# Two heads' scores in neighbouring PSUM banks with one sigmoid for both, the first mixing's products with U in four column groups, and a new table of places

## The chip, the cores and the metric

The kernel runs on one core of one Trainium2 chip, in one launch. A core has a matrix engine (TensorE, PE in the profile, with its weight loads as PEld), VectorE (DVE), ScalarE (ACT), GpSimd (POOL) and SyncE (SP), which here only issues transfers. Each engine works through its own queue in the order in which the program puts the instructions there. The metric is the device time of one execution in microseconds; lower is better. The execution that was profiled is one of its own, so its time stands beside the median of the timed runs.

## The reference, cut to what matters

Sigmoid attention for 8 samples, 12 heads of 64, 448 positions, and behind it a mixing over positions of rank 32 and a feed-forward with 768 and 3072 channels:

```python
scores = scale * np.matmul(q, k.transpose(0, 1, 3, 2)) - np.log(S)
attn = 1.0 / (1.0 + np.exp(-scores))
x = np.matmul(attn, v)              # heads side by side: 8 x 448 x 768
h = xt @ U @ V                      # xt: positions last; U 448x32, V 32x448
u = x + h.transpose(0, 2, 1)
out = u + np.maximum(u @ w_ch1, 0.0) @ w_ch2
```

The two feed-forward weights come as 64-bit words and are decoded on the chip.

## The kernel before, in words

Data lie with channels or heads on the partitions and the 448 positions along the free side. The work of a sample has three stages.

**Attention.** `pair` (line 569) takes two heads at a time, six pairs a sample. `scores_of` (L521) multiplies k and q: the two heads lie on rows 0 to 63 and 64 to 127, so that their products (L533) run in two halves of the matrix engine's rows, side by side. Each head's block of 128 keys by 448 queries fills its own PSUM bank. ScalarE drains each bank with a sigmoid of its own (L649, called in a loop over two heads at L671). `values_of` (L543) multiplies with v (L552, L562), the two heads in two halves of the columns. Samples 0 and 1 (`whole`) do this in f32. The later six, in the order of `LATER`, split every operand into two f16 parts; the attention matrix is then scaled into an f16 high part (ACT, L679) and a low part (VectorE, L680, shown by its helper's line L393).

**Mixing.** `mix(0)` (L707) serves sample 0 in f32. It transposes u by the matrix engine (L736), copies the result into one of the two buffers `XN` (ACT, L747), multiplies it with a 128-row piece of U (L748: four pieces, added up in one bank's partitions 0 to 31), copies the sum out (L765) and multiplies it with V (L773). Then u is scaled and split into `us0` (`u_parts`, L788), which is the feed-forward's input.

**Feed-forward.** Four samples run it plainly: chains of 18 products (`ffn_in`, L914), two relu drains on ACT (L921, L922) and a subtraction on VectorE (L923), then chains of 12 products (`ffn_out`, L933), each drained by one VectorE addition into u (L940, in the profile L393 with `ua`). The other four go through a Strassen-like scheme, two samples at once (L1117).

While sample 0 is in its feed-forward, `decode` (L854) turns the weights into f16 parts. A piece of 768 KB is loaded into one of the three `W64` buffers, goes through two or three VectorE operations (L393, L390), on ACT through L442 for most groups, then through an absolute sum on ACT (`bound`, L453), which gives the buffer back, and at last through a scaling on ACT or GpSimd and a subtraction on VectorE. Four pieces make a group, twelve groups make both weights.

**What sets the order.** `Plan.order` (L130) plays the program through with a cost for every operation and writes the order in which each engine gets its instructions. Among the operations that could start, the one with the smallest `pos` goes first. The positions come from the constants of lines 60 to 69. A position only sets preference: nothing waits for it.

**PSUM.** There are 8 banks of 512 f32. The feed-forward takes from banks 0 to 2 (`PF`, L320), attention from banks 3 to 7 (`PS_`); sample 0 and the first two pairs of sample 1 take scores from all eight.

Of the kernel before, what the change touches and what calls it, by code (L numbers as in the profile page):

```python
# [26 lines left out]
F32 = mybir.dt.float32  # L27
# [11 lines left out]
P = 128  # L39
D = 64  # L40
S = 448
NP = 6
RANK = 32
# [13 lines left out]
FORMS = {1: (0,), 2: (1,), 3: (2,)}  # L57
MM = 0.1893
SWITCH, BOND = 0.11, 6.0
PIPE, LANDS, LATE = 0.33e6, 3.237, 0.855  # L60

ROOM0, ROOM, AHEAD, BEFORE, PACE = 71.122, 36.236, 46.443, 36.513, 0.773
PREP, BOUNDS, VALUES, SECOND, MIXED = 17.173, 9.225, -1.615, 1.701, 4.481
MIXED1, MIX_1 = 5.441, 15.09
MIX_2, EV_IN, EV_OUT, A_OFF = 11.033, 27.459, 4.648, 3.832
START, DECODE = 67.28, 39.505
U_AT, U_STEP = 4.035, 4.181
LEAD, SUMS, STEP_K, STEP_I, FFN_LEAD = 13.145, 6.985, 47.972, 26.851, 5.28
W_AT, W_STEP, PAIR0, MIX0A, MIX0B, W2_LAG, G0_LEAD = -159.513, 5.093, 4.16, -122.622, -80.644, 0.581, 0.562
LOW_G = 1  # L70
ORDER = "iiiioiooiioiooiioiooiooo"

# [159 lines left out]
def fused_kernel(ctx: ExitStack, tc: tile.TileContext, q, k, v, wu, wv, w1, w2, out):  # L232
# [78 lines left out]
    for x, owners in ((stg, None), (at_.bitcast(F16), AT2), (US[1].ap.rearrange("p a b c -> p (a b c)"), US[1:])):  # L311
        for j in range(min(4, x.shape[1] // (2 * PIECE))):
# [3 lines left out]
                t.shares.append(o)  # L316
                o.shares.append(t)
            T32.append(t)
    BANK = [Buffer(ps.tile([P, 512], F32, name=f"bank{i}")) for i in range(8)]
    PF, PS_ = [BANK[:3]] * B, [BANK[3:]] * B  # L320
    ROW = ring("row", 1, [3 * P], F32)

    SPOT = []
# [61 lines left out]
    def pe(cost, fn, reads, writes, pos, slack=None, after=(), modes=(128, 128)):  # L385
        return op("PE", cost, fn, reads, writes, pos, LATE if slack is None else slack, 0.3, after, modes=modes)
# [118 lines left out]
    def rows_of(h):  # L505
        return slice(h * D, h * D + D)
# [14 lines left out]
    def scores_of(b, js, products, kp, pos, early):  # L521


        sc = {(j, h): plan.tile("sc", BANK if early else PS_[b], False) for j in js for h in range(2)}
        n = 1 if b < WHOLE else 3

        def fn():
            for j in js:
                for i in range(n):
                    for h in range(2):  # L530
                        if j < 3:
                            x, y = products[-1]()[i]
                            nc.tensor.matmul(sc[j, h].x[:, :S], x[rows_of(h), j * P : j * P + P], y[rows_of(h)], start=i == 0, stop=i == n - 1)  # L533
                            continue
                        for m in range(2):
                            x, y = products[m]()[i]
                            nc.tensor.matmul(sc[j, h].x[rows_of(m), :S], x[rows_of(h), 3 * P : S], y[rows_of(h)], start=i == 0, stop=i == n - 1)  # L537

        scored.append(pe(len(js) * (0.74 if b < WHOLE else 0.57) + (SWITCH if 3 in js and len(js) > 1 else 0.0), fn, kp, list(sc.values()), pos,
                         after=values_ops[-2:-1] + scored[-1:], modes=(32 if js[0] == 3 else 64, 32 if js[-1] == 3 else 64)))  # L540
        return sc

    def values_of(b, products, tiles, kp, pos, quad):  # L543
        av = plan.tile("av", PS_[b], False)
        avs = [quad["av"], av] if quad else [av]

        def fn():
            n = len(products())
            for j in range(3):
                for i, (x, y) in enumerate(products()):  # L550
                    for h in range(2):
                        nc.tensor.matmul(  # L552
                            av.x[rows_of(h), :S], x[:, j, rows_of(h)], y(tiles[j], h),
                            start=j == 0 and i == 0, stop=not quad and j == 2 and i == n - 1, skip_group_check=True,
                        )
            if not quad:
                return
            for i in range(n):
                for m in range(2):
                    x, y = quad["last"][m]()[i]  # L560
                    for h in range(2):
                        nc.tensor.matmul(avs[m].x[rows_of(h), :S], x[rows_of(m), rows_of(h)], y(tiles[3], h)[rows_of(m)],  # L562
                                         start=False, stop=i == n - 1, skip_group_check=True)

        three, one = (2.22, 0.74) if b < WHOLE else (1.71, 0.57)
        values_ops.append(pe(three + (SWITCH + one if quad else 0.0), fn, kp, avs, pos, modes=(65, 32 if quad else 65)))
        return av

    def pair(b, p, at, d):
# [92 lines left out]
        for j in range(3 + odd):  # L662
            here = at + (d * (j // 2) / SECOND if b else 0.0)
            kj = kscore + (quad["kscore"] if odd and (j == 3 or b and j == 2) else [])
            if b == 0:
                sc = scores_of(b, (j,), products, kj, here, early)
            elif j % 2 == 0:
                sc = scores_of(b, (j, j + 1) if j == 0 or odd else (j,), products, kj, here, early)
            a = tiles[j] = plan.tile("a2", A2)
            to = a if whole else plan.tile("t2", AT2)  # L670
            for h in range(2):  # L671
                cols = slice(h * S, h * S + S)
                sigmoid(0.66 if whole else 0.72, lambda to=to, cols=cols: to.x[:, cols],
                        lambda h=h, sc=sc, j=j: sc[j, h].x[:, :S], c if j < 3 or whole else cm, here, [sc[j, h]], [(to, h)])
            kto = [(to, h) for h in range(2)]
            if whole:
                keys += kto
                continue
            act(0.95, lambda a=a, to=to: nc.scalar.activation(half(a, 0), to.x, AF.Copy, scale=A_UP), kto, [(a, 0)], here + A_OFF)  # L679
            dve2(1.16, lambda a=a, to=to: rest(half(a, 1), to.x, A_UP, half(a, 0)), kto + [(a, 0)], [(a, 1)], here + A_OFF)  # L680
            keys += [(a, 0), (a, 1)]
# [25 lines left out]
    def mix(b, pos0, pos1):  # L707
# [18 lines left out]
        for hf in range(2):  # L726
# [3 lines left out]
            for sc in range(4):  # L730
# [12 lines left out]
                if whole:  # L743
                    def x32(xn=xn, w=w):
                        return xn.x.rearrange("p a b -> p (a b)").bitcast(F32)[:w]

                    act(0.48, lambda tr=tr, w=w, x32=x32: nc.scalar.copy(x32(), tr.x[:w, :384]), [tr], [xn], at)  # L747
                    pe(0.66, lambda tp=tp, w=w, sc=sc, x32=x32: nc.tensor.matmul(  # L748
                        tp.x[:RANK, :384], uraw[:w, sc], x32(), start=sc == 0, stop=sc == 3), [xn, "uraw"], [tp], at)
                    continue  # L750
                act(0.58, lambda tr=tr, xn=xn, w=w: nc.scalar.activation(xn.x[:w, 0, :], tr.x[:w, :384], AF.Copy, scale=sx.x[:w]),
                    [tr, sx], [(xn, 0)], at)
# [9 lines left out]

                pe(0.34, mixed, [(xn, 0), (xn, 1)] + KUA, [tp], at)
            if whole:
                act(0.5, lambda tp=tp, half=half: nc.scalar.copy(tt.x[:RANK, half], tp.x[:RANK, :384]), [tp], [(tt, hf)], at)  # L765
            else:
                to_t16(tp, hf, at)
        at = pos1 + (0.0 if whole else MIX_1)
        for c in range(NP):
            cut = slice(c * P, (c + 1) * P)  # L770
            lp = plan.tile("sc", BANK if b == 0 else PS_[b], False)
            if whole:
                pe(4 * MM, lambda lp=lp, cut=cut: nc.tensor.matmul(lp.x[:, :S], tt.x[:RANK, cut], vraw[:RANK], start=True, stop=True),  # L773
                   [(tt, c // 3), "vraw"], [lp], at)
                dve(0.62, lambda lp=lp, c=c: nc.vector.tensor_add(u32[c].x, lp.x[:, :S], u32[c].x), [lp, ku[c]], [ku[c]], at)
            else:
# [601 lines left out]
```

## Time and profile before

| what | us |
|---|---|
| median of 3 runs | 1550.19 (1549.12 to 1557.4) |
| the profiled execution | 1549.95 |
| its span in the profile | 1548.2 |
| TensorE matmul busy | 1526.8 |
| VectorE busy | 1119.3 |
| ScalarE busy | 846.2 |
| GpSimd busy | 388.1 |

The span runs from the first to the last instruction that the profiler saw; the profiled execution's time is 1.75 us longer. Busy time is the union of the instructions on an engine. A matmul's duration includes its way through the array, so that a chain of matmuls at 358 ns each still starts one every 189 ns; the idle time in brackets and the granted clock tell more than the busy share.

### The profile page before, as it was taken

How to read it: one execution, taken by the hardware profiler on the slowest of the kernel's cores; microseconds unless marked ns; L12 is line 12 of the kernel's file. 1: busy time of each engine (PE TensorE's matmuls, PEld its weight loads, DVE VectorE, ACT ScalarE, POOL GpSimd, SP SyncE). 2: the span in 40 equal slices, each digit the busy share in tenths (PEclk: the TensorE clock that was granted, in tenths of full speed). 3: DMA queues.
4: the chain of work that ended last, by engine and by line, in shares of the span. 5: the costliest groups of instructions: out<-in, count | busy, mean ns of one | idle time of the engine just before them, and what ended most of it. 6: DMA issues, size and time to landing. Idle time of an engine off the chain costs nothing.

```text
span 1548.2 us, 24076 instructions
## 1 busy us (share of the span) xinstructions
PE 1526.8 (99%) x8843; PEld 751.5 (49%) x8843; DVE 1119.3 (72%) x1864; ACT 846.2 (55%) x1495; POOL 388.1 (25%) x538
## 2 busy tenths in 40 slices
PE   8999989999999999999999999999999999999999
PEld 3344544544444444444444454555555555555554
DVE  4687998568776777867788757697866777565656
ACT  6788956368767667857689536342332614131310
POOL 1000010552223362323332441046454500000000
PEclk9999999999999999999999999999999999999999
DMA  8877867685664775755766566967575673443331
GB/s 235 276 264 256 293 239 256 247 257 168 178 172 130 238 205 173 203 142 149 221 205 193 181 210 217 296 204 264 179 249 170 226 257 108 122 128 108 107 108 72
DMA packets 184726, 306.02 MB, mean 198 GB/s; under 512 B 54560, under 2 KB 146080, under 8 KB 178464
## 3 DMA queue, kind: packets, MB, share of 16 engines
q1 hardware_dynamic: 184608, 304.49, 62.4%
q8 instruction: 69, 1.13, 0.3%
q14 instruction: 49, 0.40, 0.1%
HBM read 232.88 MB, written 63.26 MB: 191 GB/s over the span
## 4 chain that ended last, share of the span: by engine, by line
PE 90%; DMA 3%; DVE 3%; ACT 2%; issue 1%; SPq 0%; ACTq 0%
PE bank L1117 37%; PE bank L933 19%; PE bank L914 19%; PE bank L533 6%; PE bank L552 6%; DMA w<-w_in 1%; PE bank L562 1%; PE bank L537 1%; PE bank L829 1%; DMA qk__99<-q_in 1%; DMA v__105<-v_in 1%; ACT a L649 1%; DVE us__88 L393 1%; PE bank L838 0%; ACT w L453 0%
## 5 line engine op out<-in xcount | busy, mean ns | idle before, releaser
L933 PE MATMUL bank<-h__93,w__91 128*128 128x448 f16 x792 | 162.4, 358 | 6.5 <-DVE ua__77 L393 3.0
L933 PE MATMUL bank<-h__94,w__92 128*128 128x448 f16 x792 | 157.3, 353 | 0.6 <-DVE ua__80 L393 0.6
L393 DVE SCALAR_TENSOR_TENSOR a<-at,a 128x896 f16<-128x896 f32 x126 | 140.2, 1139 | 19.4 <-ACT a L679 18.9
L933 PEld LDWEIGHTS <-w__91 128*128 128x128 f16 x864 | 82.6, 99 | 93.9 <-issue 23.4
L914 PEld LDWEIGHTS <-w__89 128*128 128x128 f16 x864 | 84.0, 98 | 80.4 <-issue 3.8
L914 PEld LDWEIGHTS <-w__90 128*128 128x128 f16 x864 | 83.3, 98 | 81.8 <-issue 6.1
L933 PEld LDWEIGHTS <-w__92 128*128 128x128 f16 x864 | 82.6, 98 | 83.2 <-issue 9.5
L679 ACT ACTIVATE a<-at 128x896 f16<-128x896 f32 x126 | 115.1, 961 | 0.4
L976 POOL TENSOR_TENSOR w<-w 128x384 f32<-128x384 f32 x96 | 107.0, 1115 | 5.4
L1117 PEld LDWEIGHTS <-w__90 128*128 128x128 f16 x756 | 74.0, 98 | 69.0
L1117 PEld LDWEIGHTS <-w__91 128*128 128x128 f16 x756 | 74.0, 98 | 69.0
L1117 PEld LDWEIGHTS <-w__89 128*128 128x128 f16 x756 | 74.0, 98 | 69.0
L1117 PEld LDWEIGHTS <-w__92 128*128 128x128 f16 x756 | 74.0, 98 | 68.8
L914 PE MATMUL bank<-us__88,w__90 128*128 128x448 f16 x432 | 85.6, 353 | 0.0
L914 PE MATMUL bank<-us__87,w__90 128*128 128x448 f16 x432 | 85.2, 353 | 0.0
L914 PE MATMUL bank<-us__87,w__89 128*128 128x448 f16 x432 | 84.9, 353 | 0.0
L914 PE MATMUL bank<-us__88,w__89 128*128 128x448 f16 x432 | 84.8, 353 | 0.0
L533 PE MATMUL bank<-stg 64*128 64x448 f16 x648 | 74.1, 351 | 0.7 <-ACT at L649 0.7
L972 POOL TENSOR_TENSOR w<-w 128x384 f32<-128x384 f16 x48 | 45.4, 975 | 114.8 <-DVE xnt L984 80.1
L552 PE MATMUL bank<-a,stg 128*64 128x448 f16 x648 | 68.2, 355 | 0.0
L921 ACT ACTIVATE r__96<-bank 128x448 f32<-128x448 f32 x48 | 26.0, 542 | 59.3 <-PE bank L914 53.6
L649 ACT ACTIVATE at<-bank,bias_s,c__216 128x448 f32<-128x448 f32 x72 | 47.2, 727 | 18.0 <-PE bank L533 13.8
(1124 smaller groups left out, 3109.9 us busy)
## 6 DMA issues: line engine op xcount, KB each, us to landing
w<-w_in SPq DMA_DIRECT2D x48, 768.0 KB, 5.7
forms<-xnt SPq DMA_DIRECT2D x24, 768.0 KB, 4.4
w__89<-kept SPq DMA_DIRECT2D x9, 1536.0 KB, 8.7
w__90<-kept SPq DMA_DIRECT2D x9, 1536.0 KB, 6.9
w__91<-kept SPq DMA_DIRECT2D x9, 1536.0 KB, 7.5
w__92<-kept SPq DMA_DIRECT2D x9, 1536.0 KB, 8.8
w__90<-forms SPq DMA_DIRECT2D x12, 768.0 KB, 5.5
w__89<-forms SPq DMA_DIRECT2D x12, 768.0 KB, 5.5
```

The source lines that it names most:

```text
L393: nc.vector.scalar_tensor_tensor(out=out, in0=in0, scalar=s, in1=in1, op0=op0, op1=op1)
L533: nc.tensor.matmul(sc[j, h].x[:, :S], x[rows_of(h), j * P : j * P + P], y[rows_of(h)], start=i == 0, stop=i == n - 1)
L537: nc.tensor.matmul(sc[j, h].x[rows_of(m), :S], x[rows_of(h), 3 * P : S], y[rows_of(h)], start=i == 0, stop=i == n - 1)
L552: nc.tensor.matmul(av.x[rows_of(h), :S], x[:, j, rows_of(h)], y(tiles[j], h), start=j == 0 and i == 0, stop=not quad and j == 2 and i == n ...
L649: act(cost, lambda: nc.scalar.activation(out_(), in_(), AF.Sigmoid, bias=bias_s, scale=c if whole else by.x), kin + ["bias"] + ([] if whol ...
L679: act(0.95, lambda a=a, to=to: nc.scalar.activation(half(a, 0), to.x, AF.Copy, scale=A_UP), kto, [(a, 0)], here + A_OFF)
L914: nc.tensor.matmul(ph.x[:, :S], w.x[:, f, c, x], us.x[:, c, y, :], start=c == 0 and i == 0, stop=c == NP - 1 and i == 2,)
L921: act(0.54, lambda: nc.scalar.activation(r.x, ph.x[:, :S], AF.Relu, scale=DOWN_H), [ph], [r], pos - EV_IN)
L933: nc.tensor.matmul(po.x[:, :S], w.x[:, f, e, x], h.x[:, f, y, :], start=f == 0 and i == 0, stop=f == FC - 1 and i == 2,)
L972: pool(0.93, lambda j=j: nc.gpsimd.tensor_tensor(out=t.x[:, j], in0=quarter(j, 0), in1=quarter(j, 1), op=ALU.add), [w] if b is None else k ...
L976: pool(1.0, lambda o_=o_, x=x, y=y, sub=sub: nc.gpsimd.tensor_tensor(out=t.x[:, o_], in0=t.x[:, x], in1=t.x[:, y], op=ALU.subtract if sub ...
L1117: nc.tensor.matmul(bank.x[:, :S], wt[1](k, n, x), both(f)[:, y], start=start and k == i == 0, stop=k == 2 and i == 2, skip_group_check=True)
```

## The change

It has three parts.

*Scores in pairs of banks.* PSUM is now one single bank (bank0), three tiles of two neighbouring banks each (banks0 to banks2), and another single bank (bank7). A score block takes a pair: head 0 in one half, head 1 in the other. One sigmoid of 128x896 reads both halves. The feed-forward may take bank0, bank7 and the two halves of banks0. Other uses take any half of the three pairs; the value sums that open a pair of head pairs take a half of banks2.

*The first mixing.* Each of the four products with U writes to its own 32 partitions of the bank, so that each uses another group of 32 columns of the matrix engine, and none adds to another. The copy takes all 128 partitions, and the product with V contracts over 128 rows; V already lies four times below itself.

*Places.* 34 constants of the table have new values, and some planner costs follow the new operations.

```diff
-PIPE, LANDS, LATE = 0.33e6, 3.237, 0.855
+PIPE, LANDS, LATE = 0.33e6, 3.626, 0.713
...
-    BANK = [Buffer(ps.tile([P, 512], F32, name=f"bank{i}")) for i in range(8)]
-    PF, PS_ = [BANK[:3]] * B, [BANK[3:]] * B
+    BOTH = [Buffer(ps.tile([P, 2, 512], F32, name=f"banks{i}")) for i in range(3)]
+    BANK = [Buffer(ps.tile([P, 512], F32, name="bank0"))]
+    for x in BOTH:
+        for i in range(2):
+            y = Buffer(x.ap[:, i])
+            x.shares.append(y)
+            y.shares.append(x)
+            BANK.append(y)
+    BANK.append(Buffer(ps.tile([P, 512], F32, name="bank7")))
+    PF, PS_ = [[BANK[0], BANK[7], BANK[1], BANK[2]]] * B, [BANK[1:7]] * B
...
-        sc = {(j, h): plan.tile("sc", BANK if early else PS_[b], False) for j in js for h in range(2)}
+        sc = {j: plan.tile("sc2", BOTH, False) for j in js}
...
-                            nc.tensor.matmul(sc[j, h].x[:, :S], x[rows_of(h), j * P : j * P + P], y[rows_of(h)], start=i == 0, stop=i == n - 1)
+                            nc.tensor.matmul(sc[j].x[:, h, :S], x[rows_of(h), j * P : j * P + P], y[rows_of(h)], start=i == 0, stop=i == n - 1)
...
-        av = plan.tile("av", PS_[b], False)
+        av = plan.tile("av", PS_[b] if quad else BANK[5:7], False)
...
-            for h in range(2):
-                cols = slice(h * S, h * S + S)
-                sigmoid(0.66 if whole else 0.72, lambda to=to, cols=cols: to.x[:, cols],
-                        lambda h=h, sc=sc, j=j: sc[j, h].x[:, :S], c if j < 3 or whole else cm, here, [sc[j, h]], [(to, h)])
+            sigmoid(1.03 if whole else 1.13, lambda to=to: to.x.rearrange("p (h s) -> p h s", h=2),
+                    lambda sc=sc, j=j: sc[j].x[:, :, :S], c if j < 3 or whole else cm, here, [sc[j]], [(to, 0), (to, 1)])
...
-                        tp.x[:RANK, :384], uraw[:w, sc], x32(), start=sc == 0, stop=sc == 3), [xn, "uraw"], [tp], at)
+                        tp.x[sc * RANK : sc * RANK + RANK, :384], uraw[:w, sc], x32(), start=True, stop=True), [xn, "uraw"], [(tp, sc)], at)
...
-                pe(4 * MM, lambda lp=lp, cut=cut: nc.tensor.matmul(lp.x[:, :S], tt.x[:RANK, cut], vraw[:RANK], start=True, stop=True),
+                pe(4 * MM, lambda lp=lp, cut=cut: nc.tensor.matmul(lp.x[:, :S], tt.x[:, cut], vraw, start=True, stop=True),
```

What the new places do to the order shows at three places. The first is SP's queue at the program's start; `w64` is a weight piece on its way to the decoder, `qk0` and `v0` are the first pair's heads. Before:

```order
L367 DMA qk0__99<-k_in 64x448
L367 DMA qk0__99<-q_in 64x448
L367 DMA qk0__99<-k_in 64x448
L367 DMA qk0__99<-q_in 64x448
L367 DMA v0__102<-v_in 128x512
L367 DMA w64_107<-w1_in 128x6x128
L367 DMA qk1__100<-k_in 64x448
```

And now:

```order
L375 DMA w64_107<-w1_in 128x6x128
L375 DMA qk0__99<-k_in 64x448
L375 DMA qk0__99<-q_in 64x448
L375 DMA qk0__99<-k_in 64x448
L375 DMA qk0__99<-q_in 64x448
L375 DMA v0__102<-v_in 128x512
L375 DMA qk1__100<-k_in 64x448
```

The first weight piece has moved from sixth place to the front, past the first pair's five loads.

The second is ScalarE's queue at the start; `a` is the attention matrix, `ssw0` the absolute sums of a weight piece. Before:

```order
L649 ACT_TABLE_LOAD
L649 ACTIVATE a_97<-bank0_109,bias_s_64 128x448
L649 ACTIVATE a_97<-bank1_110,bias_s_64 128x448
L649 ACTIVATE a_97<-bank2_111,bias_s_64 128x448
L649 ACTIVATE a_97<-bank3_112,bias_s_64 128x448
L649 ACTIVATE a_97<-bank4_113,bias_s_64 128x448
L649 ACTIVATE a_97<-bank5_114,bias_s_64 128x448
L453 ACTIVATE w64_107,ssw0__171<-stg_108 128x768
```

And now:

```order
L461 ACT_TABLE_LOAD
L461 ACTIVATE w64_107,ssw0__168<-stg_108 128x768
L657 ACT_TABLE_LOAD
L657 ACTIVATE a_97<-banks0_109,bias_s_64 128x896
L657 ACTIVATE a_97<-banks1_110,bias_s_64 128x896
L657 ACTIVATE a_97<-banks2_111,bias_s_64 128x896
```

The piece's absolute sum, which follows that piece's decoding on VectorE, stands ahead of the first sigmoid, and a second table load stands between them.

The third is TensorE's queue late in the decoding, in sample 0's feed-forward; each row is the first of its chain, `w10` and `w11` are second weights, `h0` and `h1` the hidden parts. Before:

```order
L933 MATMUL bank1_110<-h0__93,w10__91 128x448
...
L933 MATMUL bank2_111<-h0__93,w10__91 128x448
...
L933 MATMUL bank2_111<-h1__94,w11__92 128x448
...
L933 MATMUL bank0_109<-h1__94,w11__92 128x448
...
L933 MATMUL bank1_110<-h1__94,w11__92 128x448
```

And now:

```order
L939 MATMUL bank7_113<-h0__93,w10__91 128x448
...
L939 MATMUL banks0_109<-h0__93,w10__91 128x448
...
L939 MATMUL banks0_109<-h1__94,w11__92 128x448
...
L939 MATMUL bank7_113<-h1__94,w11__92 128x448
...
L939 MATMUL bank0_112<-h1__94,w11__92 128x448
```

The chains are the same and stand in the same order; they went round three banks and now go round four, the two halves of banks0 among them.

Sample 0's first mixing also moved. Where the copy of the U products (L765, now L771) stood behind an absolute sum and before two sigmoids on ScalarE, its first half now stands directly behind one sigmoid. The products with U still stand in twos on TensorE, with a score or value step between.

More of the change, by code (lines that the diff above doesn't have):

```diff
@@ L59 @@
 SWITCH, BOND = 0.11, 6.0
-PIPE, LANDS, LATE = 0.33e6, 3.237, 0.855
[L62 to L69, printed above, removed]
+PIPE, LANDS, LATE = 0.33e6, 3.626, 0.713
+ROOM0, ROOM, AHEAD, BEFORE, PACE = 58.456, 35.051, 28.941, 21.257, 0.56
+PREP, BOUNDS, VALUES, SECOND, MIXED = 9.03, 11.55, -0.598, 3.134, 3.467
+MIXED1, MIX_1 = 5.249, 15.019
+MIX_2, EV_IN, EV_OUT, A_OFF = 10.006, 28.922, 3.918, 3.367
+START, DECODE = 67.808, 42.935
+U_AT, U_STEP = 3.868, 3.867
+LEAD, SUMS, STEP_K, STEP_I, FFN_LEAD = 12.221, 8.144, 37.395, 23.433, 3.414
+W_AT, W_STEP, PAIR0, MIX0A, MIX0B, W2_LAG, G0_LEAD = -160.588, 4.704, 4.061, -109.375, -89.47, 0.683, 0.87
 LOW_G = 1
@@ L536, in fn @@
                             x, y = products[m]()[i]
-                            nc.tensor.matmul(sc[j, h].x[rows_of(m), :S], x[rows_of(h), 3 * P : S], y[rows_of(h)], start=i == 0, stop=i == n - 1)
+                            nc.tensor.matmul(sc[j].x[rows_of(m), h, :S], x[rows_of(h), 3 * P : S], y[rows_of(h)], start=i == 0, stop=i == n - 1)
         scored.append(pe(len(js) * (0.74 if b < WHOLE else 0.57) + (SWITCH if 3 in js and len(js) > 1 else 0.0), fn, kp, list(sc.values()), pos,
@@ L747, in mix @@
                     act(0.48, lambda tr=tr, w=w, x32=x32: nc.scalar.copy(x32(), tr.x[:w, :384]), [tr], [xn], at)
-                    pe(0.66, lambda tp=tp, w=w, sc=sc, x32=x32: nc.tensor.matmul(
-                        tp.x[:RANK, :384], uraw[:w, sc], x32(), start=sc == 0, stop=sc == 3), [xn, "uraw"], [tp], at)
+                    pe(0.4, lambda tp=tp, w=w, sc=sc, x32=x32: nc.tensor.matmul(
+                        tp.x[sc * RANK : sc * RANK + RANK, :384], uraw[:w, sc], x32(), start=True, stop=True), [xn, "uraw"], [(tp, sc)], at)
                     continue
@@ L764, in mix @@
             if whole:
-                act(0.5, lambda tp=tp, half=half: nc.scalar.copy(tt.x[:RANK, half], tp.x[:RANK, :384]), [tp], [(tt, hf)], at)
+                act(0.5, lambda tp=tp, half=half: nc.scalar.copy(tt.x[:, half], tp.x[:, :384]), [(tp, x) for x in range(4)], [(tt, hf)], at)
             else:
```

## The prediction

> **What bounds the kernel now.** I read the page's head, then a table of stretches, then TensorE's waits, then the timelines of the stretches that wait.
>
> ```profile
> span 1548.2 us, 24076 instructions
> ```
>
> The columns of the stretches: length, then busy time of PE, PEld, DVE, ACT and POOL (instructions), the clock granted to PE, the DMA share and GB/s.
>
> ```profile
> 41.00:90.00 49.00, 43.84 (x185) 15.60 (x182) 36.54 (x72) 36.06 (x68) 6.62 (x6) 0.93 0.84 279
> 90.00:200.00 110.00, 110.00 (x597) 54.04 (x596) 92.21 (x164) 95.18 (x174) 0.81 (x4) 1.00 0.79 262
> 200.00:260.00 60.00, 52.95 (x263) 26.41 (x261) 52.74 (x100) 32.59 (x55) 7.34 (x11) 0.94 0.73 263
> 260.00:960.00 700.00, 699.31 (x4532) 338.35 (x4530) 519.09 (x866) 481.30 (x859) 249.73 (x389) 1.00 0.64 193
> 960.00:1548.00 588.00, 584.47 (x3109) 302.24 (x3107) 398.40 (x634) 175.22 (x295) 118.55 (x115) 1.00 0.54 175
> ```
>
> From 260 us on TensorE is never without work, 699.31 of 700 us and then to the end but for the last drains. Only removing matmul work would shorten that, and the change removes none there. So whatever ScalarE saves after 260 us is worth nothing; the time can be won or lost in the first 260 us, where PE falls idle and the clock sinks to 0.93 and 0.94. Who it waits for, total, times, longest:
>
> ```profile
> PE bank L533 <- DMA qk__99<-q_in: 4.2, 1, 4.2
> PE bank L933 <- DVE ua__77 L393: 3.0, 1, 3.0
> PE bank L933 <- DVE ua__80 L393: 2.9, 2, 2.3
> PE bank L773 <- ACT xnt L765: 1.8, 2, 1.4
> ```
>
> These are single events, each with its place, and I go through them by place. The profiled execution took 1549.95 us, span plus 1.75, and stands 0.24 below the median of 1550.19; I sum against it.
>
> **Start.** Timeline rows: start, duration, engine, line, operation, what for (idle before).
>
> ```profile
> 0.72 0.60 SPq L367 DMA_DIRECT2D qk__99<-k_in  x1
> 3.91 0.60 SPq L367 DMA_DIRECT2D w<-w_in  x1
> 9.24 0.56 DVE L390 TENSOR_SCALAR stg<-w 128x768 int32<-128x768 int32 x1 [9.24 <-DMA w<-w_in]
> 9.83 1.95 DVE L393 SCALAR_TENSOR_TENSOR stg<-w,stg 128x768 int32<-128x768 int32 x2
> 6.12 1.28 ACT L649 ACT_TABLE_LOAD   x1 [6.12 <-PE bank L533]
> 7.42 3.70 ACT L649 ACTIVATE a<-bank,bias_s 128x448 f32<-128x448 f32 x6
> 4.21 6.24 PE L533 MATMUL bank<-qk__99 64*128 64x448 f32 x12 [4.21 <-DMA qk__99<-q_in]
> ```
>
> The 768 KB piece now goes ahead of the first heads. It costs their loads one issue, about 0.6 us, and its transfer: at 279 GB/s, the rate of the stretch 41 to 90, 786 KB take 2.8 us; if the two transfers share out better, it may be under 1. PE then starts at about 7 instead of 4.21. On the other side the piece is issued 3.2 us earlier, so VectorE begins near 6.1. ScalarE now does that piece's absolute sum first: decoded at 6.1 + 0.56 + 1.95 = 8.6, sum about 1 us, another table load 1.28, so the first sigmoid starts near 10.9 instead of 7.42. PE has three score blocks to fill before it needs a pair back, and the first six single blocks took it 6.24 us, so it asks at about 13; the first double sigmoid is over near 12. That is hidden, with 1 us to spare; without that cover it would cost what the piece comes late. **Term: +3, between +1 and +5.**
>
> **One sigmoid for two heads.** Groups by line: busy, mean ns of one, idle before.
>
> ```profile
> L649 ACT ACTIVATE at<-bank,bias_s,c__216 128x448 f32<-128x448 f32 x72 | 47.2, 727 | 18.0 <-PE bank L533 13.8
> L649 ACT ACTIVATE a<-bank,bias_s 128x448 f32<-128x448 f32 x84 | 46.7, 636 | 3.3 <-PE bank L533 3.0
> L679 ACT ACTIVATE a<-at 128x896 f16<-128x896 f32 x126 | 115.1, 961 | 0.4
> L1031 ACT CAST w<-w 128x448 f16<-128x448 f32 x21 | 11.0, 574 | 0.0
> ```
>
> The trace has no sigmoid over 896. A copy over 896 takes 961 and one over 448 takes 574, so 448 more elements cost 387 ns. A double sigmoid then takes 727 + 387 = 1114 where two took 1454, and 1023 where two took 1272. Over 126 and 42 of them ScalarE saves 42.8 + 10.5 = 53 us by durations; fewer, since rows overlap. Nothing of the 42.8 counts. The 10.5 lie in the first 200 us, where ACT is busy 95.18 of 110: they are part of why I expect the waits below to shrink, and get no term of their own.
>
> **Products with U.**
>
> ```profile
> 41.34 1.48 PE L748 MATMUL bank<-xnt,uraw 128*32 128x384 f32 x4
> 69.12 1.59 PE L748 MATMUL bank<-xnt,uraw 128*32 128x384 f32 x4
> 13.54 2.48 PE L552 MATMUL bank<-a,v__102 128*64 128x448 f32 x12
> ```
>
> Two products are four records, so one takes about 0.77 us, and the eight take 6.1. Four at once can't happen: the input has two buffers, and the order shows twos. The nearest rows for two column groups at once are the value products, f32 in two halves of the columns: 2.48 us for six, 0.41 each, and 0.35 for 384 columns. That would save 8 x 0.42 = 3.3; if the groups ran one after the other, nothing. In two of the four couples the second product has 64 rows, which may not pair, so **term: -2.5, between -3.3 and 0.** The product with V keeps its columns and gets 128 rows for 32: I count it at nothing.
>
> **The wait in the first mixing.**
>
> ```profile
> 48.76 0.84 ACT L453 ACTIVATE w<-at 128x768 bf16<-128x768 f32 x1 [2.75 <-DVE at L393]
> 50.10 3.97 PE L773 MATMUL bank<-vraw,xnt 32*128 32x448 f32 x6 [1.45 <-ACT xnt L765]
> 54.62 4.06 PE L552 MATMUL bank<-a,v__103 128*64 128x448 f32 x12
> 63.44 2.48 PE L552 MATMUL bank<-a,v__104 128*64 128x448 f32 x12
> 71.29 2.52 PE L773 MATMUL bank<-vraw,xnt 32*128 32x448 f32 x6 [0.32 <-ACT xnt L765]
> ```
>
> ScalarE stood 2.75 us at an absolute sum, with the copy for L773 queued behind it; PE idled 1.45, and then ran slow: 3.97 for what took 2.52 later, 4.06 for what took 2.48. Together 1.45 + 1.45 + 1.58 = 4.5 us. In the new order that copy has a sigmoid ahead and no absolute sum, so this wait should go. What is late next is the second half's copy, which now stands behind two decoding steps on ScalarE and had only 0.32 to lose. **Term: -3, between -4.5 and 0.**
>
> The Trainium skill, TensorE: Matmul & The Clock Gate, section "Why this matters for your kernels", puts the limit at idle gaps of about 3 us. Here the trace disagrees: 1.45 us were enough. By the page the slow spells behind 1.45 and behind 2.30 below (4.7 us) would not be owed to the waits and would stay, and the forecast would be up to 4.7 us higher; I go by the rows.
>
> **From sample 0 to the feed-forward.**
>
> ```profile
> 77.65 0.32 PE L409 MATMUL bank<-ident,mm_u__156 128*128 128x128 f32 x1 [0.53 <-DVE mm_u__156 L848]
> 81.28 1.02 PE L533 MATMUL bank<-qk__100 64*128 64x448 f32 x2 [0.86 <-ACT a L649]
> 85.86 1.02 PE L533 MATMUL bank<-qk__99 64*128 64x448 f32 x2 [2.00 <-ACT a L649]
> ```
>
> Here PE waited 0.53 + 0.86 + 2.00 = 3.4 us, mostly for banks behind sigmoids. The new order puts two score blocks fewer of sample 1 and one value step fewer ahead of the first feed-forward chain, so fewer banks are asked for; but PE then reaches that chain sooner behind L409, while VectorE and ScalarE still make `us0`, and may wait for that instead. **Term: -1.5, between -3.4 and +2.**
>
> **The waits late in the decoding.**
>
> ```profile
> 206.79 2.43 PE L933 MATMUL bank<-h__93,w__91 128*128 128x448 f16 x12 [1.07 <-ACT h__94 L922]
> 212.20 3.73 PE L933 MATMUL bank<-h__93,w__91 128*128 128x448 f16 x12 [2.98 <-DVE ua__77 L393]
> 216.71 6.97 PE L933 MATMUL bank<-h__94,w__92 128*128 128x448 f16 x36 [0.56 <-DVE ua__80 L393]
> 239.62 4.70 PE L933 MATMUL bank<-h__94,w__92 128*128 128x448 f16 x24
> 251.49 6.38 PE L933 MATMUL bank<-h__93,w__91 128*128 128x448 f16 x24 [2.30 <-DVE ua__80 L393]
> 207.99 3.55 DVE L393 SCALAR_TENSOR_TENSOR us__88<-w,us__88 128x768 int32<-128x768 int32 x4
> ```
>
> PE waited 1.07 + 2.98 + 0.56 + 2.30 = 6.9 us and then ran slow, 3.73 for 2.43 and 6.38 for 4.70, another 3.0: 9.9 in all. Three of the four waits are for a feed-forward bank whose drain stands in VectorE's queue behind decoding such as the 3.55 us at 207.99. VectorE's decoding work is the same in both programs, and it is full here, 52.74 of 60. A fourth bank lets PE run one chain further ahead, 2.43 us, which covers 0.56 and 2.30 and all but 0.55 of 2.98. The 1.07 is a wait for ScalarE and stays. If no wait is long enough to slow the clock, 5.3 + 3.0 = 8.3 go. Since VectorE stays full, some of it may come back a chain later. **Term: -6, between -9.9 and 0.**
>
> **Sum.** 3 - 2.5 - 3 - 1.5 - 6 = -10, so 1549.95 - 10 = 1540. All terms at their good ends give -20.1, 1530; all at the bad ends +7, 1557.
>
> **The rivals.** *Slower: a score block finds no pair.* Before, a block needed any two of five banks, each free as soon as its own sigmoid of 727 ns was over. Now it needs two neighbouring ones, held until 1114 are over, and the feed-forward also draws on the halves of banks0. In the six later samples 72 times (four score steps for each two head pairs, three such, six samples) PE asks for one or two pairs at once, in the stretch where it now idles 0.69 of 700 us. Every wait there is pure loss. A mean wait of 0.3 us gives 21.6, hence 1562. It decides from (10 + 7.75) / 72 = 0.25 us a step. For it speaks that one pair is partly taken by value sums; against it that ScalarE has 42.8 us less to do in just these samples. The Trainium skill, TensorEngine Tiling, section "Gotcha 1: PSUM Pressure", says that row tiling, as these scores use, raises the pressure on banks; no run here shows it yet.
>
> *No change: the early waits move but do not go.* If VectorE, full from 200 to 260, and not the number of banks sets the pace, PE waits one chain later for the same drains, and the clock sinks as before. Then -6 is 0, and the first mixing's second copy takes half of the -3 back: 3 - 2.5 - 1.5 - 1.5 = -2.5, 1547.
>
> *The U products do not pair.* If f32 products in different column groups run one after the other, that part does not do what it says: 1540 + 2.5 = 1542.5.
>
> *All waits go.* 1530 to 1533, if VectorE's earlier start keeps it ahead all along.
>
> **How the numbers follow.** Forecast 0.45, no change 0.26, U alone 0.07, all waits gone 0.10, slower 0.12. About 0.5%, 7.75 us, is what a measurement of this kernel can tell from no change, so faster begins below 1542.4. Of the forecast's 0.45 I put 0.37 below that line, with 0.10 from the case without waits and 0.04 from the other two: 0.51 faster. 0.12 is slower; 0.37 lies between. The range goes from 1531 to 1557, which takes in the bounds of the terms and leaves out most of the slower rival and an edge of the best case.
>
> **What would show it.** Right: PE's first matmul near 7 us; no idle before the first products with V; 206 to 252 without a PE wait over 1 us, and the clock at 1.00 there; U couples at 0.4 us a product; ScalarE near 795 busy; 260 to 960 still full. Wrong: PE waits for ScalarE's sigmoids after 260 us, or for VectorE's `ua` additions as long as now; or a start later than 9 us.

## The result, and the profile after

| | before | after |
|---|---|---|
| median, us | 1551.8 (4 runs, 1549.12 to 1557.4) | 1589.67 (4 runs, 1588.04 to 1592.76) |
| ratio | 1 | 1.0235, 95% interval 1.0212 to 1.0259 |
| the profiled execution, us | 1549.95 | 1592.76 |

The ratio is estimated from the single runs and is not the quotient of the medians, which would be 1.0244. By it the change makes the kernel 2.35% slower. The forecast was 1540, with a range of 1531 to 1557: it is wrong, in sign too.

The head of the page after:

```profile
span 1591.0 us, 23871 instructions
PE 1527.6 (96%) x8843; PEld 749.3 (47%) x8843; DVE 1109.0 (70%) x1864; ACT 811.5 (51%) x1328; POOL 395.4 (25%) x538
```

TensorE is busy as long as before (1526.8 us then), ScalarE 34.7 us less, and yet the span is 42.8 us longer. So TensorE waits more, and the stretches show where (columns as in the prediction; the last one ends with the span):

```profile
41.00:90.00 49.00, 43.91 (x214) 16.19 (x213) 42.08 (x83) 37.81 (x59) 5.37 (x6) 1.00 0.87 294
90.00:200.00 110.00, 104.65 (x552) 49.62 (x551) 87.63 (x153) 84.91 (x149) 2.46 (x8) 0.98 0.78 255
200.00:260.00 60.00, 55.92 (x287) 28.29 (x286) 49.58 (x94) 36.46 (x59) 5.63 (x7) 0.97 0.71 257
260.00:960.00 700.00, 686.51 (x4443) 332.87 (x4442) 513.00 (x869) 447.42 (x727) 258.53 (x389) 1.00 0.63 189
960.00:1591.00 631.00, 603.87 (x3194) 308.88 (x3192) 395.71 (x636) 179.60 (x300) 117.86 (x115) 0.99 0.52 167
```

Length minus PE's busy time is its idle time. Between 260 and 960 us it rose from 0.7 to 13.5, and from 960 to the end from 3.5 to 27.1. These 36.4 us are 85% of the loss, and they lie where the prediction had put neither loss nor gain. In 200 to 260, idle time fell from 7.05 to 4.08.

TensorE's waits after: for which engine and buffer, total, times, longest.

```profile
PE banks L1123 <- DVE stg L401: 7.1, 1, 7.1
PE banks L541 <- DMA qk__99<-q_in: 7.0, 1, 7.0
PE banks L1123 <- DVE us__87 L401: 5.1, 3, 1.7
PE bank L939 <- DVE ua__79 L401: 3.0, 2, 2.3
PE banks L844 <- ACT r__96 L927: 2.5, 1, 2.5
PE bank L417 <- DVE mm_w__172 L854: 2.4, 1, 2.4
PE banks L417 <- DVE ua__75 L401: 2.1, 1, 2.1
```

Before, no wait that the profile names stood in the Strassen stage. Now some 22 us of them do (L1123), and nearly always the buffer that the waiting product writes is `banks`, a tile of two banks. The longest, 7.1 us, is only in part new: with 1.4 us just ahead of it TensorE stands 8.5 us there, and in the untied kernel below it still stands 4.9 at the same place. One of the three waits of 1.7 us shows what happens. Timeline rows after: start, duration, engine, line, operation, what for (idle before).

```profile
1365.85 0.73 PE L1123 MATMUL banks<-qk__100,w__91 128*128 128x448 f16 x3
...
1367.76 0.68 DVE L398 TENSOR_SCALAR us__87<-banks,kg__239 128x448 f32<-128x448 f32 x1 [0.83 <-PE banks L1123]
...
1370.39 0.73 PE L1123 MATMUL banks<-us__87,w__91 128*128 128x448 f16 x3
...
1371.57 0.62 DVE L401 SCALAR_TENSOR_TENSOR stg<-us__88,h__93 128x448 f32<-128x448 f32 x1
1372.10 0.68 DVE L401 SCALAR_TENSOR_TENSOR us__87<-banks,kg__239,us__87 128x448 f32<-128x448 f32 x1
...
1372.83 0.73 PE L1123 MATMUL banks<-qk__101,w__91 128*128 128x448 f16 x3 [1.71 <-DVE us__87 L401]
```

The page calls all pairs `banks`; the built program tells them apart. The product at 1372.83 writes the first half of banks2. VectorE had drained that half at 1367.76 (done at 1368.44). The product that began at 1365.85 wrote the *second* half, and its drain stands at 1372.10 in VectorE's queue, behind seven steps that have nothing to do with the new product. The new product waits for that drain, although that drain reads another bank: the built program keeps its waits for a tile as a whole, and the tile now is two banks. In the built program, 136 of TensorE's waits name an instruction that reads only the other half (66 of them at L1123, 22 at the scores L541, 14 at L939, 9 at L920); before there is none, since every bank was a tile. The planner knew nothing of it: to it the halves were separate buffers, which share only with the pair as a whole.

### The profile page after: what moved, and what is told of

Same layout as the page of the kernel before. It is cut to its first block, busy times and chain, and to the rows that moved or that the text cites. A ratio compares the mean times of both kernels' runs of the same rounds, so it can differ in the third digit from the quotient of the medians.

```text
span 1591.0 us, 23871 instructions
## 1 busy us (share of the span) xinstructions
PE 1527.6 (96%) x8843; PEld 749.3 (47%) x8843; DVE 1109.0 (70%) x1864; ACT 811.5 (51%) x1328; POOL 395.4 (25%) x538
## 4 chain that ended last, share of the span: by engine, by line
PE 74%; DVE 11%; DMA 6%; ACT 5%; issue 3%; POOL 1%; SPq 0%; DVEq 0%; ACTq 0%; POOLq 0%
PE banks L1123 23%; PE bank L939 11%; PE bank L920 10%; PE bank L1123 8%; PE banks L939 5%; PE banks L920 5%; PE banks L560 4%; PE banks L541 4%; DVE stg L401 2%; DMA w<-w_in 1%; DVE a L401 1%; DMA w<-w 1%; PE banks L570 1%; DVE at L401 1%; DVE us__88 L401 1%
## 5 line engine op out<-in xcount | busy, mean ns | idle before, releaser
L401 DVE SCALAR_TENSOR_TENSOR a<-at,a 128x896 f16<-128x896 f32 (+1 forms) x127 | 139.2, 1117 | 13.6 <-ACT a L685 12.4
L939 PE MATMUL bank<-h__93,w__91 128*128 128x448 f16 x612 | 125.2, 356 | 4.2 <-DVE ua__79 L401 3.0
L939 PEld LDWEIGHTS <-w__91 128*128 128x128 f16 x864 | 82.2, 98 | 95.8 <-issue 22.5
L920 PEld LDWEIGHTS <-w__90 128*128 128x128 f16 x864 | 84.0, 99 | 85.2 <-issue 10.0
L920 PEld LDWEIGHTS <-w__89 128*128 128x128 f16 x864 | 83.6, 98 | 83.9 <-issue 8.1
L939 PEld LDWEIGHTS <-w__92 128*128 128x128 f16 x864 | 82.8, 98 | 82.8 <-issue 8.9
L1123 PEld LDWEIGHTS <-w__90 128*128 128x128 f16 x819 | 80.1, 98 | 74.9 <-issue 0.4
L939 PE MATMUL bank<-h__94,w__92 128*128 128x448 f16 x564 | 112.9, 353 | 0.0
L1123 PEld LDWEIGHTS <-w__91 128*128 128x128 f16 x756 | 73.9, 98 | 77.9 <-issue 8.4
L1123 PEld LDWEIGHTS <-w__89 128*128 128x128 f16 x756 | 73.9, 98 | 72.6 <-issue 4.1
L1123 PEld LDWEIGHTS <-w__92 128*128 128x128 f16 x693 | 68.5, 99 | 78.6 <-issue 17.5
L541 PE MATMUL banks<-stg 64*128 64x448 f16 x648 | 73.6, 351 | 0.0
L560 PE MATMUL banks<-a,stg 128*64 128x448 f16 x648 | 68.4, 355 | 1.8 <-ACT ub__82 L695 1.6
L920 PE MATMUL bank<-us__87,w__90 128*128 128x448 f16 x306 | 62.6, 359 | 1.5 <-ACT h__93 L928 1.2
L920 PE MATMUL bank<-us__88,w__90 128*128 128x448 f16 x306 | 60.7, 353 | 0.0
L920 PE MATMUL bank<-us__88,w__89 128*128 128x448 f16 x306 | 60.6, 353 | 0.0
L939 PE MATMUL banks<-h__94,w__92 128*128 128x448 f16 x300 | 60.2, 353 | 0.3 <-ACT h__93 L928 0.3
L939 PE MATMUL banks<-h__93,w__91 128*128 128x448 f16 x252 | 50.7, 353 | 1.4 <-DVE mm_w__173 L854 1.3
L657 ACT ACTIVATE at<-banks,bias_s,c__215 128x896 f32<-128x896 f32 x36 | 38.3, 1092 | 23.2 <-PE banks L541 16.3
```

The source lines that it names most:

```text
L401: nc.vector.scalar_tensor_tensor(out=out, in0=in0, scalar=s, in1=in1, op0=op0, op1=op1)
L541: nc.tensor.matmul(sc[j].x[:, h, :S], x[rows_of(h), j * P : j * P + P], y[rows_of(h)], start=i == 0, stop=i == n - 1)
L560: nc.tensor.matmul(av.x[rows_of(h), :S], x[:, j, rows_of(h)], y(tiles[j], h), start=j == 0 and i == 0, stop=not quad and j == 2 and i == n ...
L657: act(cost, lambda: nc.scalar.activation(out_(), in_(), AF.Sigmoid, bias=bias_s, scale=c if whole else by.x), kin + ["bias"] + ([] if whol ...
L920: nc.tensor.matmul(ph.x[:, :S], w.x[:, f, c, x], us.x[:, c, y, :], start=c == 0 and i == 0, stop=c == NP - 1 and i == 2,)
L939: nc.tensor.matmul(po.x[:, :S], w.x[:, f, e, x], h.x[:, f, y, :], start=f == 0 and i == 0, stop=f == FC - 1 and i == 2,)
```

## The experiments

I held three theories against each other. **1, the tie:** the halves of a pair wait for each other, and that is the loss. **2, the places:** the new table orders the work worse. **3, the pairs** (the prediction's slower rival): score blocks wait for two neighbouring banks.

Every ratio below is to runs of the kernel before that were made in the same series; their medians were 1552.08, 1553.63 and 1553.74 us.

**Untied.** The changed kernel with every instruction in its order, and with a tile for every bank; one planned step now issues two sigmoids.

```diff
-    BOTH = [Buffer(ps.tile([P, 2, 512], F32, name=f"banks{i}")) for i in range(3)]
+    BOTH = [Buffer(Two([ps.tile([P, 512], F32, name=f"bank{2 * i + 1 + h}") for h in range(2)])) for i in range(3)]
...
+                for h in range(2):
+                    nc.scalar.activation(out_()[:, h * S : h * S + S], in_()[:, h, :S], AF.Sigmoid, bias=bias_s, scale=c if whole else by.x)
```

> The changed kernel with its places, its order of instructions and its rules for pairs, but eight PSUM tiles of one bank each instead of three tiles of two banks. One sigmoid cannot read two tiles, so it is issued as two of 128x448, one right behind the other. Theory 1 (tie): in a tile of two banks, an instruction that touches one half waits for the instructions on the other half; 136 of TensorE's waits in the built program are of that kind, 66 of them ahead of the Strassen products, and they are the loss. Then the loss goes: 1540 to 1558, the Strassen stage back from 604.8 to about 575 us. Theory 2 (places): the new table puts work in worse places: 1583 to 1593, as the changed kernel's 1589.67. Theory 3 (pairs): a score block needs two given neighbouring banks at once, and TensorE waits for them: also 1580 to 1593, since this kernel keeps that rule and gives ScalarE 53 us more to do.

Measured: 1548.93 us, ratio to before 0.9977 (0.9956 to 0.9999). Its stretches from 200 us on, and its longest waits:

```profile
200.00:260.00 60.00, 58.29 (x311) 30.38 (x309) 55.61 (x102) 42.35 (x68) 6.18 (x7) 1.00 0.72 265
260.00:960.00 700.00, 699.17 (x4533) 338.70 (x4532) 514.02 (x870) 478.50 (x855) 253.56 (x389) 1.00 0.65 197
960.00:1550.00 590.00, 581.80 (x3078) 299.90 (x3072) 389.49 (x624) 171.56 (x290) 117.77 (x115) 0.99 0.52 169
```

```profile
PE bank L549 <- DMA qk__99<-q_in: 7.2, 1, 7.2
PE bank L1133 <- ACT stg L1170: 2.7, 1, 2.7
PE bank L549 <- DVE ua__75 L791: 2.4, 1, 2.4
PE bank L949 <- DVE ua__79 L409: 2.4, 2, 1.7
PE bank L789 <- ACT xnt L781: 1.8, 1, 1.8
```

The idle time of 260 to 960 is gone (0.8 of 700), that of the end is 8.2 instead of 27.1. Theory 1 holds; 2 and 3, which left this kernel at 1580 or more, fall as causes of the loss in this order.

**The new places alone**, in the kernel before.

```diff
-ROOM0, ROOM, AHEAD, BEFORE, PACE = 71.122, 36.236, 46.443, 36.513, 0.773
+ROOM0, ROOM, AHEAD, BEFORE, PACE = 58.456, 35.051, 28.941, 21.257, 0.56
...
```

> The kernel before with nothing but the new table of places; one bank a tile, two sigmoids, the products with U as before. Theory 1 (tie): no tile has two banks, so nothing is lost: 1540 to 1560. Theory 2 (places): most of the 38 us comes here, 1575 to 1595. Theory 3 (pairs): no pairs are asked for, 1540 to 1560.

Measured: 1568.99 us, 1.0102 (1.0070 to 1.0135). None of the three theories had this number. Its longest waits:

```profile
PE bank L914 <- DVE ua__79 L393: 9.2, 1, 9.2
PE bank L533 <- DMA qk__99<-q_in: 7.0, 1, 7.0
PE bank L552 <- ACT a L649: 6.0, 2, 5.7
```

All three stand in the first 260 us. The 7.0 is the later start, which the untied kernel has too (7.2); the 9.2 is for a feed-forward bank, of which this kernel has three and not four. So the new places do harm with the old banks; with the new rules, in the untied kernel, the same places lose nothing. Which rule they need was not tried apart.

**The pairs with the old places**, the changed kernel with the table of before.

```diff
-ROOM0, ROOM, AHEAD, BEFORE, PACE = 58.456, 35.051, 28.941, 21.257, 0.56
+ROOM0, ROOM, AHEAD, BEFORE, PACE = 71.122, 36.236, 46.443, 36.513, 0.773
...
```

> The changed kernel with the old table of places: tiles of two banks, one sigmoid for two heads and the U products in four groups stay. Theory 1 (tie): the loss stays, 1575 to 1605, with waits ahead of the Strassen products like those of the changed kernel. Theory 2 (places): the loss goes, 1540 to 1558. Theory 3 (pairs): the loss stays as well, but its waits stand ahead of scores before 960 us, not in the Strassen stage.

Measured: 1586.81 us, 1.0214 (1.0180 to 1.0248). Its last stretches:

```profile
260.00:960.00 700.00, 684.23 (x4425) 333.43 (x4424) 517.95 (x864) 447.07 (x725) 260.85 (x389) 1.00 0.63 192
960.00:1582.40 622.40, 610.28 (x3257) 314.07 (x3255) 411.80 (x648) 184.41 (x307) 118.87 (x115) 1.00 0.53 172
```

The loss stays without the new places, as theory 1 has it, but it lies elsewhere than that theory expected. Idle time is 15.8 us between 260 and 960, 12.1 behind (27.1 in the changed kernel) and 25.3 in the first 260 (17.0 before). So the places decide where the loss falls. Theory 3 does not fit either: of the 15.8 us the waits at the scores (L541) are 2.5, and those at the feed-forward's chains (L920, L939) 11.4. How much of the loss is the tie in this order was not tried apart.

**The tie alone**: the kernel before, every instruction in its old order, six of its banks declared as three tiles of two.

```diff
-    BANK = [Buffer(ps.tile([P, 512], F32, name=f"bank{i}")) for i in range(8)]
+    TWOS = [ps.tile([P, 2, 512], F32, name=f"banks{i}") for i in range(3)]
+    BANK = [Buffer(ps.tile([P, 512], F32, name="bank0"))]
+    BANK += [Buffer(x[:, i]) for x in TWOS for i in range(2)]
+    BANK.append(Buffer(ps.tile([P, 512], F32, name="bank7")))
```

> The kernel before, every instruction in its old order and with two sigmoids, but six of its eight one-bank PSUM tiles are now three tiles of two banks; nothing else. Theory 1 (tie): the two halves wait for each other although nothing in the order asks for it, and the whole loss appears by itself: 1575 to 1610, with waits of TensorE spread over the Strassen products and the feed-forward. Theories 2 (places) and 3 (pairs): nothing that they speak of has changed, 1549 to 1553.

Measured: 1632.55 us, 1.0503 (1.0476 to 1.0531). Nothing but the tie differs, so the loss is the tie's; it is twice that of the change and beyond what theory 1 gave. Stretches and longest waits:

```profile
200.00:260.00 60.00, 52.70 (x274) 26.81 (x272) 51.49 (x95) 35.81 (x64) 7.33 (x11) 0.97 0.58 201
260.00:960.00 700.00, 666.91 (x4254) 322.20 (x4253) 496.95 (x842) 462.39 (x830) 237.10 (x368) 1.00 0.63 186
960.00:1636.00 676.00, 649.16 (x3485) 330.94 (x3483) 439.33 (x696) 207.97 (x346) 139.62 (x137) 1.00 0.53 171
```

```profile
PE banks L1120 <- DVE h__93 L396: 7.7, 4, 2.6
PE banks L536 <- ACT a L652: 4.8, 2, 3.8
```

Idle: 33.1 us between 260 and 960 where before had 0.7, and 26.8 behind. TensorE's busy time is also 21.7 us longer (1548.5), for which no cause was sought. Its program has 281 waits for the other half against the change's 136. Here scores, too, stand one to a half (71 of the 281 are theirs, at L536), where in the changed kernel one sigmoid reads both halves. By these counts the pairing rule takes some of the tie's price away again.

**The Strassen stage without second halves.** The changed kernel, its Strassen products on bank0, bank7 and three first halves.

```diff
-        return [plan.tile("tail", BANK, False) for _ in range(4)]
+        return [plan.tile("tail", BANK[0:1] + BANK[1:7:2] + BANK[7:8], False) for _ in range(4)]
```

> The changed kernel, but the Strassen products may only use bank0, bank7 and the first half of each pair: five banks instead of eight, and none of them tied to another. Theory 1 (tie): the time from the first to the last Strassen product, 604.8 us in the changed kernel and 573.8 before, falls by what the tie costs there, at most 31 us less, if five banks are enough: 1562 to 1578 in all. If five are too few, the stage stays at 595 to 610 and the time at 1580 to 1592; then it is the number of free banks and not the tie that counts. Theories 2 and 3: 1585 to 1595.

Measured: 1566.68 us, 1.0092 (1.0063 to 1.0120).

```profile
260.00:960.00 700.00, 685.59 (x4420) 331.85 (x4421) 509.98 (x860) 446.00 (x725) 258.18 (x389) 1.00 0.63 188
960.00:1570.00 610.00, 602.05 (x3205) 309.91 (x3202) 402.25 (x640) 179.60 (x300) 118.19 (x115) 1.00 0.54 174
```

Idle time behind 960 falls from 27.1 to 8.0, and the time by 23; before 960 it stays (14.4). Five banks that are free of each other serve this stage better than eight that are tied, and as well as eight that are not (8.2 in the untied kernel).

**The planner told.** The halves of a pair also share with each other.

```diff
+    for i in (1, 3, 5):
+        BANK[i].shares.append(BANK[i + 1])
+        BANK[i + 1].shares.append(BANK[i])
```

> The changed kernel, but the planner treats the two halves of a pair as sharing one place, as the waits do, and so hands out a half only while the other is free. Theory 1 (tie), first form: the loss comes from an order made in ignorance of the waits; told of them, the planner loses little, 1550 to 1565. Second form: it comes from having five places for single products instead of eight, and an order cannot mend that: 1575 to 1600. Theories 2 and 3: 1585 to 1595.

Measured: 1565.12 us, 1.0071 (1.0049 to 1.0093), on the line between the two forms. An order that knows of the waits wins back 24.5 of 38 us; PE's idle time is 5.1 between 260 and 960 and 8.9 behind. What is left lies in the first 260 us, where PE idles 22.9 us against 17.0 before, and in single events such as this wait for a load; fewer places may be the reason, but that was not tried apart:

```profile
PE bank L1126 <- DMA w__90<-forms: 4.3, 1, 4.3
```

**No half shared**, and the same with two sigmoids to a pair. Single products use only bank0, bank7 and the first halves, from start to end.

```diff
-    PF, PS_ = [[BANK[0], BANK[7], BANK[1], BANK[2]]] * B, [BANK[1:7]] * B
+    BANK = [BANK[i] for i in (0, 1, 3, 5, 7)]
+    PF, PS_ = [[BANK[0], BANK[4], BANK[1]]] * B, [BANK[1:4]] * B
...
```

> The changed kernel, but everything that needs one bank uses only bank0, bank7 and the first half of each pair; the second halves serve scores alone. So no instruction can wait for work in another half that it has nothing to do with, from start to end, and one sigmoid still serves two heads. Theory 1 (tie): beside the 23 us that the Strassen stage alone gave back, most of the 13.5 us for which TensorE idled between 260 and 960 us in the changed kernel go too: 1550 to 1560. If single products need more than five places before 960 us as well: 1562 to 1580.

> The same kernel with two sigmoids of 128x448 for each pair of banks, one behind the other, in the same order: ScalarE has about 53 us more to do, and a pair is held about 0.36 us longer. By the prediction's bound (what ScalarE saves after 260 us is worth nothing): as the run with one sigmoid, within 3 us. By its slower rival, that score blocks wait for a pair: longer by up to 72 x 0.36 = 26 us.

Measured: 1567.38 us, 1.0088 (1.0064 to 1.0112), with one sigmoid, and 1569.94, 1.0105 (1.0084 to 1.0126), with two. With one:

```profile
41.00:90.00 49.00, 39.04 (x160) 13.79 (x157) 36.91 (x76) 33.38 (x56) 4.20 (x6) 0.87 0.83 282
...
260.00:960.00 700.00, 696.47 (x4483) 338.26 (x4482) 511.57 (x860) 446.70 (x725) 252.18 (x386) 1.00 0.64 196
```

Between 260 and 960, 10 of the 13.5 us idle are gone, as theory 1 has it. Yet 1550 to 1560 failed, and the time is that of the other case, 1562 to 1580, in which single products need more than five places before 960 us. From 41 to 90 us, where samples 0 and 1 want banks at once, TensorE now idles 10.0 us instead of 5.1, at a clock of 0.87; in the whole of the first 260 us it idles 26.4 instead of 22.8, and behind 960 still 10.8. That five places are too few at the start fits this, but was not tried by itself. Two sigmoids cost 2.6 us more, within what the intervals leave open, and not 26: in this kernel ScalarE's time and how long a pair is held are worth next to nothing.

**The U products alone**, in the kernel before.

```diff
-                        tp.x[:RANK, :384], uraw[:w, sc], x32(), start=sc == 0, stop=sc == 3), [xn, "uraw"], [tp], at)
+                        tp.x[sc * RANK : sc * RANK + RANK, :384], uraw[:w, sc], x32(), start=True, stop=True), [xn, "uraw"], [tp], at)
...
```

> The kernel before with the four products with U in four groups of 32 columns, each on its own 32 partitions, and the product with V over 128 rows; order and everything else as before. By the working of the prediction a product falls from 0.77 us to about 0.4 where two stand side by side: 0 to 3.3 us less, 1546.5 to 1550.5. If the groups do not run side by side: 1549 to 1551.5, and a couple of products still takes 1.5 us. None of the three theories puts a loss here.

Measured: 1553.03 us, 1.0000 (0.9978 to 1.0022). In microseconds that is above both ranges, since the kernel before stood at 1552.08 itself in this series. Two couples, which took 1.48 and 1.59 us before:

```profile
42.53 0.84 PE L748 MATMUL bank<-xnt,uraw 128*32 128x384 f32 x4
...
45.01 1.59 PE L748 MATMUL bank<-xnt,uraw 128*32 128x384 f32 x4
```

The first couple falls from 1.48 to 0.84, and the second stays: it is the one whose second product has 64 rows. Two of four couples pair: 1.3 us, too little to measure.

**Two tries at a better kernel**, both from the untied one. The first has the old places of the first weight piece and of the Strassen stage; the second also lets the second group's input forms in three products earlier.

```diff
-U_AT, U_STEP = 3.868, 3.867
-LEAD, SUMS, STEP_K, STEP_I, FFN_LEAD = 12.221, 8.144, 37.395, 23.433, 3.414
+U_AT, U_STEP = 4.035, 4.181
+LEAD, SUMS, STEP_K, STEP_I, FFN_LEAD = 12.221, 6.985, 47.972, 26.851, 3.414
...
-            fs = u_forms(b0, b1, su, at - LEAD, [begun[-8]])
+            fs = u_forms(b0, b1, su, at - LEAD, [begun[-11]])
```

> The untied kernel (two sigmoids, eight one-bank tiles) with the old places of the first weight piece and of the Strassen stage (U_AT, U_STEP, SUMS, STEP_K, STEP_I, and W_AT at -159.5). In the untied kernel the first matmul stood at 7.21 us instead of 4.21, and a stall of 8.1 us, less 0.6 of work in it, stood between 1217 and 1227 us. Theory 1 with the forecast's terms for the first 260 us right: both go, 1548.9 - 3 - 6 = 1540, 1537 to 1546. If the new places are needed as a whole: 1546 to 1560.

> The untied kernel with the old places of the start and the Strassen stage, and the second group's input forms let in three products earlier (about 5 us). There GpSimd had idled 20.9 us until 1202.4 and then stood ahead of the VectorE steps for which TensorE waited 4 us near 1224 to 1229 us. If that wait is all that keeps this kernel from the forecast: 1543 to 1548, that is 0.993 to 0.997 of before. If the places only move the stall: 1549 to 1556.

Measured: 1551.51, 0.9989 (0.9973 to 1.0005), and 1550.04, 0.9978 (0.9964 to 0.9993). Both times lie in the second case of their expectations. The first matmul is back at 4.16 us in the first, but a new wait of 3.7 us for a load, up to 26.84 us, took that gain back. The stall near 1224 us is 3.3 and 0.7 us of waits in the first; the longest waits of the second:

```profile
PE bank L549 <- DMA qk__99<-q_in: 6.7, 2, 4.1
PE bank L549 <- DMA qk__100<-q_in: 2.0, 1, 2.0
PE bank L425 <- DVE mm_w__175 L864: 1.3, 1, 1.3
PE bank L1133 <- ACT a L1170: 1.2, 1, 1.2
```

The stall is down to 1.2 and 0.7 there, and the time did not follow, so that wait was not all that kept this kernel from the forecast.

This one and the untied kernel are the two that beat both before and after, before by 0.2%, with intervals that just leave out no difference; neither reaches the forecast.

## Why the prediction was wrong

**The step that failed** is the first one: "Only removing matmul work would shorten that, and the change removes none there. So whatever ScalarE saves after 260 us is worth nothing; the time can be won or lost in the first 260 us". That a gain after 260 us was closed off is right, and the pair of runs with one and with two sigmoids bears it out. That nothing could be *lost* there does not follow: an engine that never waits can be made to wait. I weighed that once, for the scores, and took the halves of a pair for separate banks, as the planner does. The Strassen stage, which was full and was to use six halves, did not come up at all, and in this order it has most of the loss: 23 us of 38 went when its products were kept off the second halves. The text's own sign for being right, "260 to 960 still full", failed with 13.5 us of idle time.

**The slower rival** named waits for banks after 260 us, and the time leaned its way, past its 1562. Its mechanism was not the one: untied, the score blocks still need their pairs and TensorE idles 0.8 us in 700, and in the kernel without shared halves, with a pair held about 0.36 us longer, the time moves by 2.6 us. The clause in it that "the feed-forward also draws on the halves of banks0" was nearest to the cause.

**The terms**, which lie in the first 260 us:

- *Start, +3:* right. The first matmul stands at 7.02 us, 2.81 later.
- *One sigmoid, worth nothing to the end:* right (the pair of runs above). Sizes: estimated 1114 and 1023 ns, measured

```profile
L657 ACT ACTIVATE a<-banks,bias_s 128x896 f32<-128x896 f32 x42 | 39.8, 1007 | 3.3 <-PE banks L541 3.1 <-PE banks L545 0.2
L657 ACT ACTIVATE at<-banks,bias_s,c__213 128x896 f32<-128x896 f32 x36 | 38.6, 1094 | 11.9 <-PE banks L541 8.8 <-DVE a L401 1.9 <-issue 1.3
```

  ScalarE's busy time fell by 34.7 us and not by 53. Back to back, rows overlap: before, 72 single sigmoids of 727 ns are 52.3 us by their mean and 47.2 by their busy time.
- *U products, -2.5:* mis-sized; 1.3 us, since only the couples of 128 rows pair.
- *First mixing, -3:* right on its own wait, not on the gain. The first copy's wait of 1.45 us became 0.58 in the changed kernel and went in the untied one. In the changed kernel the slow running behind it went too (2.48 for what took 4.06), but a wait of 2.4 us for `mm_w__172` that no term had stands behind it. In the untied one a wait of 2.4 for `ua__75` brought the slow running back (clock 0.66 from 50 to 60 us, as before), and the second copy became late, 1.8, as the text feared. That 1.45 us were enough to cause the slow running, as the term has it, does not hold as a rule (last section).
- *From sample 0 to the feed-forward, -1.5:* about right in the changed kernel, where 1.7 us of waiting (L417, for `mm_u__153`) stand in place of 3.4.
- *Late decoding, -6:* right in mechanism, hidden by the tie. In 200 to 260, PE's idle time went from 7.05 us to 1.71 and the clock from 0.94 to 1.00 in the untied kernel; in the changed one only to 4.08, at 0.97.

In sum, idle time in the first 260 us went from 17.0 us before (4.8, 5.2, 0 and 7.05 by stretch) to 22.8 in the changed kernel and 16.9 untied, with about 3 of start in both. The forecast's -10 for this part was too good even without the tie: untied, the whole time came down by 0.23%, some 3.6 us. One thing stays open: a stall of some microseconds between about 1217 and 1260 us in the kernels with the new rules or the new places, tied or not. Where it is a wait for VectorE and ScalarE it was followed only as far as VectorE's steps that stand behind GpSimd's for the second group; with the planner told and with no half shared it is a wait of 4.3 us for a load.

## What to carry to other kernels

Before two buffers are joined in one tile to save an instruction, ask who else uses the halves: waits may be kept for the tile, so that a product waits for a drain it has nothing to do with, and a planner that counts the halves as free does not see it. "This engine is never idle there" excludes a gain from the others' savings, never a loss. Keeping the second halves for the scores alone, or telling the planner, gave back about two thirds here, and leaving the tiles apart gave back all.

## What the runs showed of the hardware

The matmuls behind a wait can run slow. One chain of 24 met a wait in three kernels: untied, before, and changed.

```profile
247.11 4.70 PE L949 MATMUL bank<-h__93,w__91 128*128 128x448 f16 x24 [1.71 <-DVE ua__79 L409]
```

```profile
251.49 6.38 PE L933 MATMUL bank<-h__93,w__91 128*128 128x448 f16 x24 [2.30 <-DVE ua__80 L393]
```

```profile
250.76 6.38 PE L939 MATMUL bank<-h__93,w__91 128*128 128x448 f16 x24 [2.30 <-DVE ua__79 L401]
```

Behind 1.71 us the chain runs at full speed; behind 2.30 it takes 1.7 us longer. But the runs give no limit by length. Here is a chain of 18 in the kernel of pairs with the old places, and the first mixing's products with V in the run of the U products alone:

```profile
353.06 3.57 PE L920 MATMUL bank<-us__88,w__89 128*128 128x448 f16 x18 [2.52 <-DVE ua__79 L401]
```

```profile
51.33 2.52 PE L773 MATMUL bank<-vraw,xnt 128*128 128x448 f32 x6 [2.11 <-ACT xnt L765]
```

Behind 2.52 us the chain of 18 takes 3.57, where another takes 3.56 behind 0.16. Behind 2.11 us the products with V take 2.52, the full speed, where the kernel before took 3.97 behind 1.45 at the same place. So a wait of about 2 us may or may not have a slow stretch behind it, and what decides it was not found. The prediction weighed the Trainium skill, TensorE: Matmul & The Clock Gate, section "Why this matters for your kernels", with its limit at idle gaps of about 3 us, against 1.45 us in the first mixing. Slow stretches did follow gaps below the page's figure, 1.45 and 2.30; that such a gap is enough does not follow, as 2.11 and 2.52 show.

Two f32 products of 128 rows in neighbouring groups of 32 columns start 6 ns apart and take 0.84 us for the two instead of 1.48; with 64 rows in the second they run one after the other, 1.59 us as in one group.
